# A long convolution with routed experts: output and scores by step of the last stage, one transfer for a step's tables

## The chip, the cores and the metric

The kernel runs on one core of a Trainium2 chip. The metric is the device time of one execution in microseconds, as the median of several runs. One further execution was recorded by the hardware profiler; all rows below come from that one.

## The reference

Two things are computed one after the other, for 8 sequences of 6336 positions with 128 features each.

1. A causal convolution along the sequence, each feature with its own filter: `y = irfft(rfft(x, 2S) * rfft(h, 2S))[:S]`.
2. A layer of experts on the result. Every position gets a score, `scores = y @ w_gate`. In each sequence the 128 positions with the largest scores are replaced by `y + sigmoid(score) * (relu(y @ w1) @ w2)`; `w1` is 128 x 1024 and `w2` 1024 x 128. All other positions keep `y`.

```
out = y.copy()
for b in range(8):
    top = argpartition(-scores[b], 128)[:128]
    out[b, top] += sigmoid(scores[b, top]) * (relu(y[b, top] @ w1) @ w2)
```

## The kernel before

The transform of length 6400 = 50 x 128 is done by matrix products. A sequence pair or a single sequence is worked on as a "unit"; there are 8, numbered 0 to 7. In units 0 to 5 two units belong to a pair of sequences, and each holds half of the features; units 6 and 7 are single sequences. Unit -1 is the filter.

A unit passes through four stages, all of them products on PE with copies or sums behind them:

- **a** (`products_a`, L194; copies by ACT or the DVE, L211): 8 blocks of x, each in two halves. x is loaded by `load_x` (L126), and each block is folded by two sums before use (`fold`, L133 and L134, on the DVE or POOL).
- **b** (`stage_b`, products recorded under the helper's line L109): 13 chunks. Each needs a table (`tab_wb`, L156) and the filter's spectrum (`hd`, L162 or L165). The DVE multiplies (L276 or L282), POOL adds (L287).
- **c** (`stage_c`, L300; copies by ACT, L301): 16 chunks.
- **d**, the last stage (`stage_d`, L320): 8 steps. A step takes two tables of 200 KB (`load_d`, L172, `tab_at`), makes 16 products into two banks, `pt[0]` and `pt[1]`, copies the first bank to SBUF on ACT (L324, tile `st`), and forms sum and difference on the DVE (L329, L330). Then POOL multiplies by the gate weights (L338, tile `tm`), and `rest` reduces that to scores in the tile `ss` on the DVE (L356 for units 0 to 5, L348 to L354 for units 6 and 7) and issues two stores of 200 KB on SP's queue (L359), each of 4 KB from 50 lanes. `rest` is put off to the next step (one step later still in unit 7).

The tiles `st`, `tm`, `tx`, `cmp` and a few others share one ring of 5 buffers (`wide`), so a new `st` waits until an old one has been stored. In unit 7 `st` lies elsewhere, in `reg`.

Stages of different units are interleaved by a list written ahead (`plan`): the d-steps of a unit run between the a-blocks of the unit after next (two halves of a block, then one d-step), and the c-chunks of a unit between the b-chunks of the next. In unit 6 the d-steps run between c-chunks of unit 7, and those of unit 7 alone.

All ordinary transfers are issued by SP, in the order of the program. Tables lie in a ring `wbuf` of six slots of 2 KB per lane (`room`): a d-step takes two neighbouring slots, a b-chunk two (three or none in units 6 and 7), a chunk of the filter one. `ask` looks ahead in the plan and issues loads as long as the users between the current one and the one asked for hold no more than six slots:

```
if sum(1 if o[0] == "j" else 0 if o in own else 3 if o[0] == "b" and o[1] >= SINGLE else 2
       for o in users[used:asked[0] + 1]) > 6:
    break
tabs[s] = (load_d if s[0] == "d" else load_b)(*s[1:])
```

For a d-step in the midst of its stage that means: tables are asked for two steps ahead. A load waits in SP's queue until the slot's last reader is done, and whatever stands behind it waits with it.

The search for the 128 largest scores (`keys` with L375 to L385, `search` with L416 to L505) turns scores to whole-number keys and narrows a threshold digit by digit: comparisons on the DVE (L464, L466) and ACT (L477), counts over the lanes by a small product on PE. For units 0 to 5 it runs piece by piece between the steps of later units; for units 6 and 7 serially. `places` works out the rows' numbers, POOL gathers them from the output (L622), the experts run, and POOL scatters them back (L668). The number of a row counts positions of a lane in the order in which the scores of the lane lie in `ss`, and `rows_out` views the output in the same order.

Of the kernel before, what the change touches and what calls it, by code (L numbers as in the profile page):

```python
# [7 lines left out]
F32 = mybir.dt.float32  # L8
# [4 lines left out]
ALU = mybir.AluOpType  # L13
AX = mybir.AxisListType
# [3 lines left out]
B, S, D = 8, 6336, 128  # L18
N1, N2 = 50, 128
L = N1 * N2  # L20
HD = D // 2
# [3 lines left out]
LN = 114  # L25
# [8 lines left out]
def conv_moe(ctx, tc, x, h, w_gate, w1, w2, fa_d, wb_d, wc_d, at_d, tri_d, cst_d, outs):  # L34
    nc = tc.nc
    v = nc.vector
    g = nc.gpsimd
    cp = ctx.enter_context(tc.tile_pool(name="cp", bufs=1))
# [18 lines left out]
    def single():  # L57
        return turn(banks)
# [5 lines left out]
    def wide(name):  # L64
        return tp.tile([128, 1024], F32, tag="t", name=name, bufs=5)

    def small(shape, dtype, name, bufs=1):
        return tp.tile(shape, dtype, tag=name, name=name, bufs=bufs)
# [6 lines left out]
    def sums(unit):  # L75
        t = big[:, 0:2 * 128 * HD] if unit + 1 == NU else half
        return t.rearrange("p (j r m t) -> p j r m t", j=HD, r=2, t=2)
# [9 lines left out]
    cst = cp.tile([128, 14], F32, name="cst")  # L87
# [5 lines left out]
    lane16 = (lanes16[0:LN, 0:1], lanes16[0:LN, 1:2])  # L93
    wbuf = cp.tile([128, 6 * KC * 128], F32, name="wbuf")
    hd = dp.tile([2, 128, 2 * N1 * HD], F32, name="hd")
    ss = [cp.tile([LN, 2, 2, 32], F32, name="ss%d" % i) for i in range(2)]

    def view(unit):
        if unit >= SINGLE:
# [36 lines left out]
    used_room = [0]  # L136

    def room(n):
        o = used_room[0] % 6
        used_room[0] += n  # L140
        return wbuf[:, o * 512:(o + n) * 512]
# [24 lines left out]
        return wt, [ht[:, r * kn * HD:(r + 1) * kn * HD] for r in range(2)]  # L166

    def load_d(unit, i):
        r = []
        for c in range(2):  # L170
            t = room(1)[:, 0:8 * N1].rearrange("p (c a r n) -> p c a r n", c=2, a=2, r=2)
            nc.sync.dma_start(out=t, in_=at_d[:, i, 2 * c:2 * c + 2])  # L172
            r.append(t)
        return r
# [134 lines left out]
    def flush(keep=0):  # L309
        while len(late) > keep:  # L310
            late.pop(0)()

    def stage_d(unit, i, ats):
        u, hv = unit % 2, sums(unit)
        pt = [single(), single()]
        for r in range(2):
            for c in range(4):
                for a in range(2):
                    m = 8 * i + 4 * a + c
                    nc.tensor.matmul(pt[r][a * 64:a * 64 + N1, c * 128:c * 128 + 128],  # L320
                                     ats[c // 2][0:LN, c % 2, a, r], hv[0:LN, :, r, m], start=True, stop=True)
# [12 lines left out]
        n = D if unit >= SINGLE else HD  # L334
        split = last and i > 6
        for e, o in ((g, 0), (v, 512)) if split else ((g, 0),):
            z = 512 if split else 1024
            e.tensor_tensor(out=tm[:, o:o + z].rearrange("p (a d) -> p a d", d=n),  # L338
                            in0=st[:, o:o + z].rearrange("p (a d) -> p a d", d=n),
                            in1=w.unsqueeze(1).broadcast_to([LN, z // n, n]), op=ALU.mult)  # L340

        def rest():
            if unit >= SINGLE:
                tv = tm.rearrange("p (s c d) -> p s c d", s=2, c=4)
                k = 0 if unit + 1 < NU else 3 if split else 1
                for c in range(k):
                    for a in range(1 if split else 2):
                        nc.scalar.activation(out=small([LN, D], F32, "tossed"), in_=tv[:, a, c], func=AF.Copy,  # L348
                                             accum_out=ss[u][:, 0, a, 4 * i + c:4 * i + c + 1])
                if split:  # L350
                    v.tensor_reduce(out=ss[u][:, 0, 1, 4 * i:4 * i + 4], in_=tv[:, 1], axis=AX.X, op=ALU.add)
                    v.tensor_reduce(out=ss[u][:, 0, 0, 4 * i + k:4 * i + 4], in_=tv[:, 0, k:4], axis=AX.X, op=ALU.add)
                else:
                    v.tensor_reduce(out=ss[u][:, 0, :, 4 * i + k:4 * i + 4], in_=tv[:, :, k:4], axis=AX.X, op=ALU.add)  # L354
            else:
                v.tensor_reduce(out=ss[u][:, :, :, 4 * i:4 * i + 4].rearrange("p b s c -> p s c b"),  # L356
                                in_=tm.rearrange("p (s c b d) -> p s c b d", s=2, c=4, b=2), axis=AX.X, op=ALU.add)
            for a in range(2):
                nc.sync.dma_start(  # L359
                    out=outs[unit][a, :, :, 4 * i:4 * i + 4],  # L360
                    in_=st[a * 64:a * 64 + N1].rearrange("p (s c b d) -> p s c b d", s=2, c=4, b=2))

        late.append(rest)

    def keys(units, nb, bits):

        key = small([LN, 2, nb, HD], F32, "key%d" % nb)
        tmp = spare[0:LN, 48:432] if nb == 2 else wide("keys")[0:LN, 0:384]  # L370
        tmp = tmp.bitcast(I32)
        ki, hf = tmp[:, 0:64 * nb], tmp[:, 128:128 + 128 * nb].rearrange("p (h b n) -> p h b n", h=2, b=nb)
        tot = ss[units[0] % 2][:, 0:nb].rearrange("p b s c -> p (b s c)")
        if nb == 2:
            v.tensor_tensor(out=tot, in0=tot, in1=ss[1].rearrange("p b s c -> p (b s c)"), op=ALU.add)  # L375
        raw = tot.bitcast(I32)
        v.tensor_scalar(out=ki, in0=raw, scalar1=31, scalar2=-2147483648, op0=ALU.arith_shift_right,
                        op1=ALU.bitwise_or)
        v.tensor_tensor(out=ki, in0=ki, in1=raw, op=ALU.bitwise_xor)
        kb = ki.rearrange("p (b n) -> p b n", b=nb)  # L380
        v.tensor_scalar(out=hf[:, 0], in0=kb, scalar1=bits, scalar2=2 ** (32 - bits) - 1,
                        op0=ALU.logical_shift_right, op1=ALU.bitwise_and)
        v.tensor_scalar(out=hf[:, 1], in0=kb, scalar1=2 ** bits - 1, scalar2=None, op0=ALU.bitwise_and)
        kv = key.rearrange("p h b (s c) -> p (h b) s c", s=2)
        v.tensor_tensor(out=kv, in0=hf.rearrange("p h b (s c) -> p (h b) s c", s=2),  # L385
                        in1=cst[0:LN, 5:7].unsqueeze(1).unsqueeze(3).broadcast_to([LN, 2 * nb, 2, 32]), op=ALU.mult)
        return key

    share = [7]
# [3 lines left out]
    def search(units, paced):  # L393
# [15 lines left out]
        if paced:  # L409
            key = keys(units, nb, bits)  # L410
            yield "v"
        else:
            ahead = small([LN, nt], F32, "ahead")
            limits = small([LN, 2], F32, "limits")
            v.memset(bb, 0.5)
            v.scalar_tensor_tensor(out=nth, in0=row, scalar=-float(base ** levels[0] // base),  # L416
                                   in1=bb.unsqueeze(2).broadcast_to([LN, nb, nt]), op0=ALU.mult, op1=ALU.add)
            key = keys(units, nb, bits)
            yield "v"
# [177 lines left out]

    def rows_out(unit):
        if unit >= SINGLE:
            return outs[unit].rearrange("a n s c b d -> (a n s c) (b d)")  # L600
        return outs[unit].rearrange("a n s c b d -> (a n s c b) d")

    w1s = (big[:, 16384:16896], half[:, 1024:1536])
    w2s = half[:, 0:1024]
# [25 lines left out]
    def expert(n, units, iu):  # L630
# [27 lines left out]
        def finish():  # L658
            v.scalar_tensor_tensor(out=xe, in0=py[:, 0:D], scalar=gg[:, 0:1], in1=xe, op0=ALU.mult, op1=ALU.add)
            for i, u in enumerate(units):  # L660
                back.append((rows_out(u), iu, xe[:, i * wd:i * wd + wd]))
# [71 lines left out]
    for u in range(NU):  # L733
        if u + 2 <= NU:
            both = merge(c_list(u), b_list(u + 1))
            n = next(i for i, s in enumerate(both) if s[0] == "b") + 2 * (u % 2)
# [76 lines left out]
    for s in plan:  # L813
        kind, unit = s[0], s[1]
        n = (unit + 1) * 8
# [5 lines left out]
        if kind == "a":  # L821
            q, t = s[2:]
# [22 lines left out]
        elif kind == "j":  # L845
            c = s[2]
# [8 lines left out]
            n = KCH[c][1] * HD  # L855
# [16 lines left out]
        elif kind == "c":  # L872
            stage_c(*s[1:])
            i = HALVES.index(s[2] // 2 * 2)
# [157 lines left out]
```

## Time and profile before

| | |
|---|---|
| Median of 3 runs | 797.8 us (797.77 to 798.41) |
| The profiled execution's own time | 804.7 us |
| Span of the profiled execution, first to last instruction | 802.8 us |
| Mean granted TensorE clock | 0.983 of full speed |
| PE, PEld, DVE, ACT, POOL busy | 92%, 80%, 78%, 56%, 69% of the span |
| Bytes moved | 157.64 MB, 196 GB/s on average |

The engines are PE (TensorE's products), PEld (its weight loads, beside the products), DVE (VectorE), ACT (ScalarE), POOL (GpSimd) and SP (SyncE, which only issues transfers here). Times in rows are microseconds from the start of the span; L172 is line 172 of the kernel before. In rows of the timeline, "[1.28 <-DMA wbuf<-tab_at]" says that the engine stood idle for 1.28 us just before and that a transfer into `wbuf` ended most of it; "issue" there is idle time for which the profile shows no releaser. A tile's name stands for all its buffers.

### The profile page before, as it was taken

To read this page: it belongs to the slowest core of one execution; us is meant where nothing else is said; L and a number is where in the kernel's file an instruction comes from. 1 tells how busy PE (TensorE), PEld (TensorE's weight loads), DVE (VectorE), ACT (ScalarE), POOL (GpSimd) and SP (SyncE) were. 2 spreads that over 40 slices of the span, in tenths; PEclk is the share of its full clock that TensorE was granted. 3 is DMA by queue.
4 is the path that set the end of the run, shared out by engine and by line. 5 is a ranking of instruction groups with operands and counts; after the bars stand their busy time and mean duration, and the time that the engine had idled before them with its cause. 6 is when DMAs were issued, how large, how long until landed. Compare 5 with 4: busy or idle time off the path is not lost.

```text
span 802.8 us, 39710 instructions
## 1 busy us (share of the span) xinstructions
PE 735.0 (92%) x17566; PEld 643.2 (80%) x17566; DVE 629.7 (78%) x1067; ACT 451.5 (56%) x965; POOL 551.3 (69%) x406
## 2 busy tenths in 40 slices
PE   6699979999999999999999999999999998888665
PEld 6675578888999878987889788889888888778554
DVE  5549956676767699999877898999668997975983
ACT  4687643365336546666456466655554666655562
POOL 0018928977797779877978698777885666722933
PEclk9889989999999999999999999999999999999989
DMA  7829816657865776578647774699478736521610
GB/s 268 259 83 329 267 55 215 208 166 233 261 216 160 231 261 215 155 219 273 229 126 230 256 259 123 193 331 327 126 224 267 253 110 183 171 65 31 205 54 17
DMA packets 82292, 157.64 MB, mean 196 GB/s; under 512 B 9366, under 2 KB 30088, under 8 KB 82120
## 3 DMA queue, kind: packets, MB, share of 16 engines
q1 hardware_dynamic: 81224, 154.05, 59.4%
q8 instruction: 138, 2.26, 1.1%
q0 software_dynamic: 896, 1.05, 0.5%
q14 instruction: 34, 0.28, 0.1%
HBM read 121.77 MB, written 33.29 MB: 193 GB/s over the span
## 4 chain that ended last, share of the span: by engine, by line
PE 65%; DVE 18%; issue 7%; DMA 5%; ACT 2%; POOL 1%; SPq 1%; another core or an unknown queue 0%; POOLq 0%; DVEq 0%; ACTq 0%
PE pb L300 23%; PE pt L109 17%; PE pb L320 10%; PE pt L194 10%; DVE tx L282 2%; DVE cmp L464 2%; PE pb L109 2%; PE pb L194 1%; PE pm L109 1%; DVE ss L354 1%; DVE st L329 1%; DVE st L330 1%; DMA out<-st 1%; ACT junk L477 1%; DVE st L251 1%
## 5 line engine op out<-in xcount | busy, mean ns | idle before, releaser
L301 ACT COPY half<-pb 114x512 f32<-114x512 f32 x224 | 147.0, 656 | 165.5 <-PE pb L300 161.1
L287 POOL TENSOR_TENSOR big<-big,tx 128x512 f32<-128x512 f32 (+1 forms) x104 | 132.0, 1302 | 77.5 <-DVE tx L282 68.0
L338 POOL TENSOR_TENSOR tm<-st,wg 114x1024 f32<-114x1024 f32 x56 | 133.8, 2392 | 63.4 <-DVE st L330 41.7
L287 POOL TENSOR_TENSOR reg<-reg,tx 128x512 f32<-128x512 f32 (+1 forms) x104 | 130.8, 1291 | 48.2 <-PE pb L300 28.5
L300 PE MATMUL pb<-wc,reg 128*50 128x64 f32 x4096 | 126.4, 220 | 4.1 <-issue 3.7
L300 PEld LDWEIGHTS pb<-wc,reg 128*50 128x50 f32 x4096 | 121.8, 126 | 7.7 <-issue 5.7
L300 PEld LDWEIGHTS pb<-wc,big 128*50 128x50 f32 x4096 | 118.5, 126 | 3.0 <-ACT reg L211 0.3
L300 PE MATMUL pb<-wc,big 128*50 128x64 f32 x4096 | 120.6, 219 | 0.1
L320 PE MATMUL pb<-half,wbuf 114*50 114x128 f32 x1792 | 112.2, 274 | 5.7 <-issue 2.1
L320 PEld LDWEIGHTS pb<-half,wbuf 114*50 114x50 f32 x1792 | 97.1, 123 | 12.9 <-issue 3.2
L109 PE MATMUL pt<-big,wbuf 128*64 128x256 f32 x704 | 87.4, 388 | 0.8 <-issue 0.6
L109 PE MATMUL pt<-reg,wbuf 128*64 128x256 f32 x704 | 85.1, 388 | 0.0
L211 ACT COPY reg<-pt 128x800 f32<-128x800 f32 x64 | 56.3, 928 | 44.4 <-PE pt L194 44.3
L282 DVE TENSOR_TENSOR tx<-pt,wbuf 128x1024 f32<-128x1024 f32 (+1 forms) x65 | 76.3, 1174 | 0.0
L329 DVE TENSOR_TENSOR st<-pb,st 114x512 f32<-114x512 f32 x56 | 38.6, 689 | 47.4 <-PE pb L320 32.4
L109 PEld LDWEIGHTS pt<-big,wbuf 128*64 128x64 f32 x704 | 57.7, 135 | 19.5 <-issue 1.1
L109 PEld LDWEIGHTS pt<-reg,wbuf 128*64 128x64 f32 x704 | 52.3, 135 | 20.9
L211 ACT COPY big<-pt 128x800 f32<-128x800 f32 x59 | 51.6, 931 | 22.6 <-PE pt L194 20.7
L356 DVE TENSOR_REDUCE ss<-tm 114x16 f32<-114x1024 f32 x48 | 58.4, 1216 | 7.2 <-POOL tm L338 6.5
L282 DVE TENSOR_TENSOR reg<-pt,wbuf 128x1024 f32<-128x1024 f32 (+1 forms) x39 | 45.9, 1178 | 18.6 <-PE pt L109 18.4
L194 PE MATMUL pt<-fa,big 50*64 50x100 f32 x2336 | 59.4, 249 | 0.0
L194 PEld LDWEIGHTS pt<-fa,big 50*64 50x64 f32 x2336 | 51.9, 133 | 6.3 <-issue 3.5
(175 smaller groups left out, 1206.0 us busy)
## 6 DMA issues: line engine op xcount, KB each, us to landing
wbuf<-tab_at SPq DMA_DIRECT2D x128, 200.0 KB
out<-st SPq DMA_DIRECT2D x112, 200.0 KB
wbuf<-tab_wb SPq DMA_DIRECT2D x84, 256.0 KB
wbuf<-hd SPq DMA_DIRECT2D x84, 256.0 KB
big<-in_x SPq DMA_DIRECT2D x37, 512.0 KB
half<-in_x SPq DMA_DIRECT2D x15, 512.0 KB
hd<-st SPq DMA_DIRECT2D x24, 256.0 KB
reg<-in_x SPq DMA_DIRECT2D x12, 512.0 KB
```

Of the source, the lines that this page charges most:

```text
L109: nc.tensor.matmul(out[lo:hi], w[:, lo:hi], r, **k)
L194: nc.tensor.matmul(o, w, tab[lanes, c], start=True, stop=True)
L211: nc.scalar.copy(out=o, in_=i)
L282: v.tensor_tensor(out=dst.rearrange("p h a j k t -> p k h a j t"), in0=src, in1=w, op=ALU.mult)
L287: g.tensor_tensor(out=yv[:, :, r], in0=yv[:, :, r], in1=zv[:, :, 1 - r], op=ALU.add if r else ALU.subtract)
L300: nc.tensor.matmul(pt[i2 * 64:i2 * 64 + N1, o:o + HD], w, wc[:, i2], start=True, stop=True)
L301: nc.scalar.copy(out=hv[0:LN, c * 4 + j:c * 4 + j + 2].rearrange("p j r m t -> p (j r) t m"), in_=pt[0:LN].rearrange("p (j t m) -> p j t m ...
L320: nc.tensor.matmul(pt[r][a * 64:a * 64 + N1, c * 128:c * 128 + 128], ats[c // 2][0:LN, c % 2, a, r], hv[0:LN, :, r, m], start=True, stop=True)
L329: v.tensor_tensor(out=st[:, 0:512], in0=pt[1][0:LN], in1=st[:, 512:1024], op=ALU.add)
L338: e.tensor_tensor(out=tm[:, o:o + z].rearrange("p (a d) -> p a d", d=n), in0=st[:, o:o + z].rearrange("p (a d) -> p a d", d=n), in1=w.unsq ...
L356: v.tensor_reduce(out=ss[u][:, :, :, 4 * i:4 * i + 4].rearrange("p b s c -> p s c b"), in_=tm.rearrange("p (s c b d) -> p s c b d", s=2, c ...
L464: v.tensor_tensor(out=cv, in0=cur.unsqueeze(2).broadcast_to([LN, nb, nv, HD]), in1=nth[:, :, 0:nv].unsqueeze(3).broadcast_to([LN, nb, nv, ...
```

## The change

Three things change together.

- The output of a unit is laid out as (half, lane, step, s, c, b, d) instead of (half, lane, s, step and c, b, d). What a step stores for a lane is then one run of 4 KB in DRAM, and not two of 2 KB.
- The score tile `ss` gets the same order (step, s, c) within a lane, with the reductions, the keys and the mask in L385 rewritten for it, since the rows' numbers follow it. `rows_out` and the reordering after the launch follow too.
- `load_d` loads a step's tables by one transfer of 400 KB into two neighbouring slots, unless the ring stands at its last slot; then it loads two halves as before.

```
-    ss = [cp.tile([LN, 2, 2, 32], F32, name="ss%d" % i) for i in range(2)]
+    ss = [cp.tile([LN, 2, 8, 2, 4], F32, name="ss%d" % i) for i in range(2)]
...
     def load_d(unit, i):
+        if used_room[0] % 6 < 5:
+            t = room(2)[:, 0:16 * N1].rearrange("p (c a r n) -> p c a r n", c=4, a=2, r=2)
+            nc.sync.dma_start(out=t, in_=at_d[:, i])
+            return [t[:, 0:2], t[:, 2:4]]
         r = []
         for c in range(2):
             t = room(1)[:, 0:8 * N1].rearrange("p (c a r n) -> p c a r n", c=2, a=2, r=2)
...
-                v.tensor_reduce(out=ss[u][:, :, :, 4 * i:4 * i + 4].rearrange("p b s c -> p s c b"),
+                v.tensor_reduce(out=ss[u][:, :, i].rearrange("p b s c -> p s c b"),
                                 in_=tm.rearrange("p (s c b d) -> p s c b d", s=2, c=4, b=2), axis=AX.X, op=ALU.add)
             for a in range(2):
                 nc.sync.dma_start(
-                    out=outs[unit][a, :, :, 4 * i:4 * i + 4],
+                    out=outs[unit][a, :, i],
                     in_=st[a * 64:a * 64 + N1].rearrange("p (s c b d) -> p s c b d", s=2, c=4, b=2))
...
-        kv = key.rearrange("p h b (s c) -> p (h b) s c", s=2)
-        v.tensor_tensor(out=kv, in0=hf.rearrange("p h b (s c) -> p (h b) s c", s=2),
-                        in1=cst[0:LN, 5:7].unsqueeze(1).unsqueeze(3).broadcast_to([LN, 2 * nb, 2, 32]), op=ALU.mult)
+        kv = key.rearrange("p h b (i s c) -> p (h b i) s c", s=2, c=4)
+        v.tensor_tensor(out=kv, in0=hf.rearrange("p h b (i s c) -> p (h b i) s c", s=2, c=4),
+                        in1=cst[0:LN, 5:7].unsqueeze(1).unsqueeze(3).broadcast_to([LN, 16 * nb, 2, 4]), op=ALU.mult)
...
-        return outs[unit].rearrange("a n s c b d -> (a n s c b) d")
+        return outs[unit].rearrange("a n i s c b d -> (a n i s c b) d")
...
-    args.append([nc.dram_tensor("out_%d" % u, (2, N1, 2, 32, 2, HD), F32, kind="ExternalOutput").ap()
+    args.append([nc.dram_tensor("out_%d" % u, (2, N1, 8, 2, 4, 2, HD), F32, kind="ExternalOutput").ap()
```

The reductions for units 6 and 7 (L348 to L354) and the sum of two units' scores (L375) are reindexed in the same way, with the same sizes.

## Rows read from the trace of the kernel before

**Rows 1.** The page: busy time by engine, and the chain's shares by engine.
```profile
PE 735.0 (92%) x17566; PEld 643.2 (80%) x17566; DVE 629.7 (78%) x1067; ACT 451.5 (56%) x965; POOL 551.3 (69%) x406
...
PE 65%; DVE 18%; issue 7%; DMA 5%; ACT 2%; POOL 1%; SPq 1%; another core or an unknown queue 0%; POOLq 0%; DVEq 0%; ACTq 0%
```
**Rows 2.** Timeline of PE, last stage of unit 1 (start, us, engine, line, operation).
```profile
251.53 1.60 PE L194 MATMUL pt<-fa,reg 50*64 50x100 f32 x64
253.07 1.97 PE L320 MATMUL pb<-half,wbuf 114*50 114x128 f32 x32
254.96 1.60 PE L194 MATMUL pt<-fa,reg 50*64 50x100 f32 x64
```
**Rows 3.** Stretches: us, busy time by engine (PE first), PEclk, DMA share, GB/s.
```profile
248.10:277.40 29.30, 28.02 (x775) 25.40 (x774) 18.72 (x22) 19.13 (x25) 21.31 (x12) 1.00 0.71 215
574.00:608.80 34.80, 33.26 (x932) 30.40 (x928) 23.10 (x39) 20.86 (x28) 27.22 (x16) 0.95 0.60 180
```
**Rows 4.** Timeline of SP's issues, last stage of unit 1.
```profile
254.95 1.72 SPq L172 DMA_DIRECT2D wbuf<-tab_at  x2
256.76 1.68 SPq L359 DMA_DIRECT2D out<-st  x2
258.54 1.94 SPq L172 DMA_DIRECT2D wbuf<-tab_at  x2
```
**Rows 5.** Who waited for the tables, then for the stores (us, times).
```profile
  PE pb L320: 2.7, 4
...
  ACT st L324: 9.2, 5
```
**Rows 6.** SP's instructions by line: ns min/median/max, first and last start.
```profile
L255 SPq DMA_DIRECT2D hd<-st x26: 319/418/1886, 51.8 to 97.1; - x26
...
L172 SPq DMA_DIRECT2D wbuf<-tab_at x128: 327/425/1869, 157.5 to 752.7; - x128
...
L359 SPq DMA_DIRECT2D out<-st x112: 777/809/1257, 172.4 to 699.3; - x112
```
**Rows 7.** Timeline of the DVE, last stage of unit 4.
```profile
509.72 0.69 DVE L329 TENSOR_TENSOR st<-pb,st 114x512 f32<-114x512 f32 x1 [0.16 <-ACT st L324]
```
**Rows 8.** Timeline of PE, idle times in the last stages of units 0 and 1.
```profile
180.33 1.92 PE L320 MATMUL pb<-half,wbuf 114*50 114x128 f32 x30 [0.42 <-issue]
...
194.84 1.97 PE L320 MATMUL pb<-half,wbuf 114*50 114x128 f32 x32 [0.69 <-DVE st L330]
...
272.72 1.30 PE L320 MATMUL pb<-half,wbuf 114*50 114x128 f32 x20 [1.27 <-issue]
```
**Rows 9.** Timeline of SP's issues, last stage of unit 5.
```profile
570.67 8.73 SPq L126 DMA_DIRECT2D big<-in_x  x2
579.45 3.79 SPq L172 DMA_DIRECT2D wbuf<-tab_at  x6
```
**Rows 10.** Timeline of PE, last stage of unit 5.
```profile
583.66 0.65 PE L320 MATMUL pb<-half,wbuf 114*50 114x128 f32 x8 [1.28 <-DMA wbuf<-tab_at]
584.56 2.40 PE L320 MATMUL pb<-half,wbuf 114*50 114x128 f32 x24 [0.26 <-DMA wbuf<-tab_at]
586.89 2.34 PE L194 MATMUL pt<-fa,reg 50*64 50x100 f32 x64
```
**Rows 11.** Stretch of 2 us in unit 5, columns as in group 3.
```profile
586.00:588.00 2.00, 2.00 (x38) 1.65 (x38) 0.90 (x2) 0.00 (x0) 1.32 (x2) 0.50 0.77 250
```
**Rows 12.** Timelines of SP, PE and the DVE, last stage of unit 7.
```profile
752.14 2.11 SPq L172 DMA_DIRECT2D wbuf<-tab_at  x2
...
752.96 1.96 PE L320 MATMUL pb<-big,wbuf 114*50 114x128 f32 x32 [0.67 <-DMA wbuf<-tab_at]
...
757.26 1.52 PE L320 MATMUL pb<-big,wbuf 114*50 114x128 f32 x24 [0.45 <-DMA wbuf<-tab_at]
...
758.89 0.69 DVE L329 TENSOR_TENSOR reg<-pb,reg 114x512 f32<-114x512 f32 x1 [0.36 <-ACT tossed L348]
```
**Rows 13.** The DVE's operation that masks the keys, L385: ns min/median/max.
```profile
L385 DVE TENSOR_TENSOR key<-keys,cst x2: 293/294/294, 703.4 to 764.3; 114x128 f32<-114x128 int32 x2
```

More of the change, by code (lines that the diff above doesn't have):

```diff
@@ L348, in rest @@
                         nc.scalar.activation(out=small([LN, D], F32, "tossed"), in_=tv[:, a, c], func=AF.Copy,
-                                             accum_out=ss[u][:, 0, a, 4 * i + c:4 * i + c + 1])
+                                             accum_out=ss[u][:, 0, i, a, c:c + 1])
                 if split:
-                    v.tensor_reduce(out=ss[u][:, 0, 1, 4 * i:4 * i + 4], in_=tv[:, 1], axis=AX.X, op=ALU.add)
-                    v.tensor_reduce(out=ss[u][:, 0, 0, 4 * i + k:4 * i + 4], in_=tv[:, 0, k:4], axis=AX.X, op=ALU.add)
+                    v.tensor_reduce(out=ss[u][:, 0, i, 1], in_=tv[:, 1], axis=AX.X, op=ALU.add)
+                    v.tensor_reduce(out=ss[u][:, 0, i, 0, k:4], in_=tv[:, 0, k:4], axis=AX.X, op=ALU.add)
                 else:
-                    v.tensor_reduce(out=ss[u][:, 0, :, 4 * i + k:4 * i + 4], in_=tv[:, :, k:4], axis=AX.X, op=ALU.add)
+                    v.tensor_reduce(out=ss[u][:, 0, i, :, k:4], in_=tv[:, :, k:4], axis=AX.X, op=ALU.add)
             else:
-                v.tensor_reduce(out=ss[u][:, :, :, 4 * i:4 * i + 4].rearrange("p b s c -> p s c b"),
+                v.tensor_reduce(out=ss[u][:, :, i].rearrange("p b s c -> p s c b"),
                                 in_=tm.rearrange("p (s c b d) -> p s c b d", s=2, c=4, b=2), axis=AX.X, op=ALU.add)
@@ L372, in keys @@
         ki, hf = tmp[:, 0:64 * nb], tmp[:, 128:128 + 128 * nb].rearrange("p (h b n) -> p h b n", h=2, b=nb)
-        tot = ss[units[0] % 2][:, 0:nb].rearrange("p b s c -> p (b s c)")
+        tot = ss[units[0] % 2][:, 0:nb].rearrange("p b i s c -> p (b i s c)")
         if nb == 2:
-            v.tensor_tensor(out=tot, in0=tot, in1=ss[1].rearrange("p b s c -> p (b s c)"), op=ALU.add)
+            v.tensor_tensor(out=tot, in0=tot, in1=ss[1].rearrange("p b i s c -> p (b i s c)"), op=ALU.add)
         raw = tot.bitcast(I32)
@@ L599, in rows_out @@
         if unit >= SINGLE:
-            return outs[unit].rearrange("a n s c b d -> (a n s c) (b d)")
-        return outs[unit].rearrange("a n s c b d -> (a n s c b) d")
+            return outs[unit].rearrange("a n i s c b d -> (a n i s c) (b d)")
+        return outs[unit].rearrange("a n i s c b d -> (a n i s c b) d")
     w1s = (big[:, 16384:16896], half[:, 1024:1536])
@@ L1021 @@
     o = _np.stack([r.results[0]["out_%d" % u] for u in range(NU)])
-    w = o[0:n].reshape(n // 2, 2, 2, N1, 2, 8, 4, 2, HD).transpose(0, 7, 2, 3, 4, 5, 6, 1, 8)
-    w = _np.concatenate([w.reshape(n, 2, N1, 2, 8, 4, D), o[n:].reshape(B - n, 2, N1, 2, 8, 4, D)])
+    w = o[0:n].reshape(n // 2, 2, 2, N1, 8, 2, 4, 2, HD).transpose(0, 7, 2, 3, 5, 4, 6, 1, 8)
+    ones = o[n:].reshape(B - n, 2, N1, 8, 2, 4, D).transpose(0, 1, 2, 4, 3, 5, 6)
+    w = _np.concatenate([w.reshape(n, 2, N1, 2, 8, 4, D), ones])
     y = _np.zeros((B, N1, N2, D), o.dtype)
```

## Prediction

> **What bounds the kernel now.** I read the parts by engine and by chain first. The span is 802.8 us, PE is busy for 735.0 of it, and the chain of work that ended last runs through PE for 65% and through DMA for 5% [rows 1]. The change touches nothing of PE's work, only stores, table loads and the order of 64 scores in a lane, so its gain can only come out of the few stretches in which PE or the DVE waits for SP's queue. To find them I read the stretches that hold the last stage, which runs 8 steps per unit (a step here: two products of the unit after next, L194, and then the 16 products of the last stage, L320).
>
> A step without a stall takes 3.43 us: L194 starts at 251.53 and again at 254.96 [rows 2]. Eight of them are 27.4 us. In the stretch of unit 1 PE is busy 28.02 of 29.30 us, in that of unit 5, the longest, 33.26 of 34.80 [rows 3]. So all that such a stage could give back is 1 to 2 us, unit 5 apart.
>
> Next SP's queue, in order of time. In these stages it issues without a pause: two table loads 1.72 us, two stores 1.68 us, the next two loads 1.94 [rows 4]. That is 3.4 to 3.6 us a step, PE's own pace, so SP, once late, stays late. The reader should see that SP is nearly as full as PE, and that this alone costs nothing: what counts is who waits for what it issues. Waits of PE for the tables are four in the whole span, 2.7 us together. Waits for the stores fall on ACT, which needs an st buffer back: five, 9.2 us [rows 5].
>
> **The change, part by part.**
>
> *Stores (L359), 128 of them.* Each moves the same 200 KB; a lane's 4 KB become one run instead of two of 2 KB. Its issue costs SP 777 ns at least and 809 at the median, where a store of 128 lanes with one run each (hd) costs 418 and a table load 425 [rows 6]. The new store has one run per lane, so I take 418 ns. Its bounds are 319, the lowest of the hd store, and 809, if the price hangs on the 50 lanes and not on the runs. Two stores per step: 0.84 us for 1.68. A page of the Trainium skill speaks against the change here: "DMA: Bandwidth & Descriptors", section "Why a DMA increments its semaphore by 16 and not by 1", says that a transfer runs on the largest number of engines, up to 16, that divides the slowest dimension of both sides. By that rule 50 lanes run on 10 engines before and after, and a price that hangs on the lanes would stay: 1.68 us a step, the first rival below. No row here tells engines apart.
>
> *Table loads (L172), 128 of them.* Two of 200 KB become one of 400 KB where two neighbouring slots of the ring of six are left. Counting the slots through the plan (1 for a "j", 2 for a "b" or "d", 3 or none for a "b" of units 6 and 7), the ring stands at its last slot in three steps of every unit but unit 5: 21 steps stay split, 43 are merged, and 85 issues remain. Merged: 425 ns for about 1.7 us of back-to-back issue, bounds 327 and 1,700 (the time for the bytes of both). SP's step falls from 3.4 or more to 0.84 + 0.43 = 1.3 us, at worst 1.68 + 1.7 = 3.4, as now. The price: the first half can't start before both slots are free, nor be used before all 400 KB are there. SP waits for the second slot anyway before it goes on, so only the landing counts. In an undisturbed stage tables are asked for two steps ahead, 6.9 us; that is the cover. Where SP was blocked it is gone, which is unit 5, below.
>
> *Where late stores cost.* ACT's 9.2 us come mostly in units 2 and 4, where the search keeps the DVE busy. Behind a copy that one of these waits held up, the DVE had stood idle for 0.16 us [rows 7]. It is the DVE's own list of work that PE then waits for, and an earlier store doesn't shorten it. I take 0.2 us for all, bounds 0 and 0.9 (0.16 and the 0.69 that PE waits for DVE's L330 in unit 0 [rows 8]).
>
> *Stalls of PE with no releaser.* 0.42 us in unit 0 and 1.27 in unit 1 are marked "issue" [rows 8]: the profile shows nothing that they wait for, so I give the change nothing of them; bounds 0 and 1.7.
>
> *Unit 5, second step.* SP's queue was in the x loads from 570.67 to 579.40, held there by the second, and issued the tables of three steps from 579.45 [rows 9]. PE was ready at 582.4, got the first half at 583.66 and the second at 584.56 [rows 10]. The clock then fell: 24 pieces of L320 took 2.40 us (0.10 each, against 1.97 for 32, 0.062 each [rows 2]), 64 of L194 2.34 against 1.60, at a granted clock of 0.50, the lower level of 1.2 GHz, in 586 to 588 [rows 10, 11]. Merged, the block in the x loads stays, and the tables' bytes queue behind the same x load. The whole lands about when the second half did, 0.2 us earlier for one issue less, but the 8 pieces that ran on the first half (0.65 us) now run after it. Net +0.4 us; bounds -0.5 and +1.9 (second rival).
>
> *Unit 7.* SP issues the last step's tables at 752.14 for 2.11 us, and PE's last 24 pieces wait 0.45 us for them, the step before 0.67 [rows 12]. With SP at 1.3 us a step both go. But the DVE is full there: before the last sum it stood idle 0.36 us [rows 12]. So 0.4 us of the 1.1 reach the end, with 0.36 taken; bounds 0 and 1.1. The search that follows is serial, so this lies on the path in full.
>
> *Scores.* The order inside a lane changes from (s, i, c) to (i, s, c); all sums and compares keep their sizes. Only L385 walks in runs of 4 instead of 32, five times, 294 ns in units 6 and 7 and on the path there once [rows 13]. Taken 0; bounds 0 and +0.3, doubling it. Gathers and scatters at the end address rows of the same size.
>
> **Sum.** -0.2 (stores) +0.4 (unit 5) -0.4 (unit 7) = -0.2 us, to which I add half of PE's stall of 0.69 in unit 0 and nothing else: -0.5 us. The profiled execution took 804.7 us (its span and 1.9 around it), so 804.2; the median of the runs is 797.8, 0.9% below, and the same 0.5 us leaves 797.3. What covers the 2 us of issue that each step saves is PE, 96% busy in the stage; were PE faster, SP would be the next in line.
>
> **Rivals.**
>
> *Stores no cheaper (no effect).* If the issue price belongs to the 50 lanes, a store stays at 0.81 us and only the loads gain. SP still drops to 2.1 us a step. Against it: nothing but the two rows of 128 lanes. The time is then 797.8 less half of the 0.5, 797.6.
>
> *SP's relief is paid in full (faster).* If the late tables, the st buffers and the unexplained stalls all hang on the full queues, then 2.7 (tables) + 0.92 and 0.74 (pieces at the lower clock, 2.40 - 1.48 and 2.34 - 1.60) + 0.69 + 1.69 = 6.7 us are to be had. Half of it, 3.4, gives 794.4. For it: SP is full and every one of these stalls lies in the last stage. Against it: only 2.7 us are put down to tables, and the DVE covers part. The same page's section "Rules for kernel authors" asks to coalesce many small transfers into large ones, and so speaks for this case; no row here shows how much it is worth.
>
> *The merged table comes late (slower).* In unit 5 nothing covers the load. If 400 KB land later than 585.5, 1 us after the second half now, PE loses this 1.0, and the 8 pieces that ran ahead now cost 0.8 at the lower clock: +1.8 us. With unit 7's gain at its bound of 0 that is 799.6, and up to 801 if the third step's tables, next in the queue, are late as well. For it: the wait is at the worst place, behind an x load of 512 KB. Against it: the bytes ahead of the second half are the same as now.
>
> **How the numbers follow.** A measurement of this kernel tells 0.2%, 1.6 us, from no change. Forecast 797.3 with 0.34 and the rival without cheaper stores with 0.12 lie within it: same 0.46. Paid in full 0.36: faster. Late merged table 0.18: slower. The bounds of the terms add up to -4.2 (0.9 + 1.7 + 0.5 + 1.1) and +2.2 (1.9 + 0.3) around 797.8, so 793.6 to 800.0. I take 794.0 to 800.0; what lies past 794.4 in the second rival and the far end of the third stay outside. The forecast's own range is 796.2 to 799.4.
>
> **What would show it.** Right: stores with one run issue in about 0.42 us, 85 table loads, SP with pauses in the last stages, the stage of unit 1 still at 29 us, PE's waits for tables in unit 7 gone, DVE there as full as now. Wrong: the stage of units 0 to 4 shorter by over 1 us each, PE's "issue" stalls gone, or the clock at the higher level through unit 5. A wait at 583 that grew past 3 us would show the slow rival.

## The result, and the profile after

The changed kernel takes 803.45 us (median of 22 runs, 795.34 to 808.81) where the kernel before takes 797.79 us in the same number of runs (789.73 to 800.18). The ratio is 1.006, with a 95% interval of 1.0036 to 1.0084: it is slower, by about 5 us. The ratio leaves out the two longest runs of the changed kernel (808.33 and 808.81 us), which count as a slow state; the medians of all runs stand at 1.007. The prediction was 797.3 us in a range of 794.0 to 800.0. Both the sign and the range were wrong.

One warning before the rows. Single executions of either kernel differ by 10 us and more. The profiled execution of the changed kernel took 799.85 us, 3.6 us below its median; that of the kernel before took 804.7, 6.9 us above. So the two spans (798.1 and 802.8 us) stand the wrong way round, and a comparison of whole profiles would call the change a gain. What can be compared is stages, and what recurs over many profiles.

In the changed kernel L194 is L198, L320 is L324, L324 is L328, L359 is L363, L385 is L389; the merged table load is L171 and the split one L176. First the page's parts 1 and 4 of the changed kernel, against [rows 1]:

```profile
PE 732.4 (92%) x17566; PEld 634.8 (80%) x17566; DVE 629.2 (79%) x1067; ACT 451.9 (57%) x965; POOL 551.4 (69%) x406
...
PE 66%; DVE 18%; issue 6%; DMA 5%; ACT 3%; POOL 1%; SPq 0%; POOLq 0%; DVEq 0%; ACTq 0%
```

Nothing shows at this distance. SP's instructions by line (ns min/median/max) say that the issue became cheap, as forecast [rows 6]:

```profile
L171 SPq DMA_DIRECT2D wbuf<-tab_at x43: 327/363/1883, 158.1 to 740.8; - x43
...
L176 SPq DMA_DIRECT2D wbuf<-tab_at x42: 327/363/1722, 158.5 to 745.4; - x42
...
L363 SPq DMA_DIRECT2D out<-st x112: 285/326/1749, 170.5 to 698.9; - x112
```

SP's timeline of unit 1 after, against [rows 4], has the pauses too: a merged load and two stores are 1.1 us of a step of 3.43. Over the whole of that stage SP is issuing for 24.0 of 27.7 us before and for 12.9 of 25.8 after.

```profile
251.06 0.69 SPq L363 DMA_DIRECT2D out<-st  x2
252.53 1.49 SPq L176 DMA_DIRECT2D wbuf<-tab_at  x2
254.48 0.69 SPq L363 DMA_DIRECT2D out<-st  x2
256.40 0.36 SPq L171 DMA_DIRECT2D wbuf<-tab_at  x1
257.92 0.75 SPq L363 DMA_DIRECT2D out<-st  x2
```

PE's step in that stage is what it was [rows 2]; its timeline:

```profile
252.86 1.60 PE L198 MATMUL pt<-fa,reg 50*64 50x100 f32 x64
254.39 1.97 PE L324 MATMUL pb<-half,wbuf 114*50 114x128 f32 x32
256.29 1.60 PE L198 MATMUL pt<-fa,reg 50*64 50x100 f32 x64
```

The waits (total us, times, longest) show that ACT waits half as long for the stores [rows 5], and PE somewhat longer for the tables (POOL's waits for stores, not among those rows, went the other way, from 3.5 to 8.2 us):

```profile
ACT st L328 <- DMA out<-st: 4.8, 4, 2.4
PE pb L324 <- DMA wbuf<-tab_at: 3.5, 3, 2.3
```

PE's timeline in the last stages of units 0 to 5 holds what had not been foreseen: six idle times marked "issue", 4.8 us together, where the kernel before had three (0.42, 1.27 [rows 8] and one of 0.21).

```profile
173.52 0.90 PE L198 MATMUL pt<-fa,big 50*64 50x100 f32 x28 [0.19 <-issue]
...
188.57 0.91 PE L198 MATMUL pt<-fa,big 50*64 50x100 f32 x30 [0.97 <-issue]
...
420.74 0.65 PE L324 MATMUL pb<-half,wbuf 114*50 114x128 f32 x8 [0.75 <-issue]
...
431.26 0.47 PE L198 MATMUL pt<-fa,big 50*64 50x100 f32 x9 [1.46 <-issue]
...
509.77 0.40 PE L198 MATMUL pt<-fa,big 50*64 50x100 f32 x7 [0.85 <-issue]
...
599.45 0.39 PE L198 MATMUL pt<-fa,big 50*64 50x100 f32 x3 [0.57 <-issue]
```

In unit 5 SP is blocked in the x loads for as long as before [rows 9], and PE waits for the whole merged table [rows 10]; in this execution the clock stayed up (PEclk, the third figure from the end in the row of the stretch, is 1.00 where it was 0.95 [rows 3]):

```profile
570.58 8.71 SPq L126 DMA_DIRECT2D big<-in_x  x2
579.39 2.84 SPq L171 DMA_DIRECT2D wbuf<-tab_at  x3
...
584.60 1.96 PE L324 MATMUL pb<-half,wbuf 114*50 114x128 f32 x32 [2.35 <-DMA wbuf<-tab_at]
586.50 1.60 PE L198 MATMUL pt<-fa,reg 50*64 50x100 f32 x64
...
574.00:608.80 34.80, 31.89 (x934) 29.26 (x930) 23.13 (x40) 21.03 (x28) 27.36 (x16) 1.00 0.63 193
```

In unit 7 one of the two waits for tables is left, 0.51 us, and the DVE's last sum starts without a pause [rows 12]; the masking of the keys costs the same [rows 13]:

```profile
746.95 4.01 PE L324 MATMUL pb<-big,wbuf 114*50 114x128 f32 x64 [0.51 <-DMA wbuf<-tab_at]
...
752.60 0.68 DVE L333 TENSOR_TENSOR reg<-pb,reg 114x512 f32<-114x512 f32 x1
...
754.04 1.86 DVE L342 TENSOR_TENSOR reg<-reg,wg 114x512 f32<-114x512 f32 x1
...
L389 DVE TENSOR_TENSOR key<-keys,cst x2: 291/292/293, 703.6 to 758.5; 114x128 f32<-114x128 int32 x2
```

And the DMA queues (packets, MB, share of 16 engines' span), first the kernel before, then the changed one: 15% fewer packets in q1, the queue of SP's transfers, and the same share of time. The queue q8, whose kind is "instruction", will be needed below.

```profile
q1 hardware_dynamic: 81224, 154.05, 59.4%
q8 instruction: 138, 2.26, 1.1%
```

```profile
q1 hardware_dynamic: 68632, 154.05, 59.4%
q8 instruction: 138, 2.26, 1.1%
```

### The profile page after: what moved, and what is told of

The parts are those of the page before. It is cut to its first block, busy times and chain, and to the rows that moved or that the text cites. A ratio compares the mean times of both kernels' runs of the same rounds, so it can differ in the third digit from the quotient of the medians.

```text
span 798.1 us, 39624 instructions
## 1 busy us (share of the span) xinstructions
PE 732.4 (92%) x17566; PEld 634.8 (80%) x17566; DVE 629.2 (79%) x1067; ACT 451.9 (57%) x965; POOL 551.4 (69%) x406
## 3 DMA queue, kind: packets, MB, share of 16 engines
q1 hardware_dynamic: 68632, 154.05, 59.4%
## 4 chain that ended last, share of the span: by engine, by line
PE 66%; DVE 18%; issue 6%; DMA 5%; ACT 3%; POOL 1%; SPq 0%; POOLq 0%; DVEq 0%; ACTq 0%
PE pb L304 22%; PE pt L109 17%; PE pt L198 11%; PE pb L324 11%; DMA wbuf<-tab_at 2%; DVE cmp L468 2%; DVE tx L286 2%; PE pb L109 2%; ACT junk L481 2%; PE pb L198 1%; PE pm L109 1%; DVE ss L358 1%; DVE st L333 1%; DVE st L334 1%; DMA out<-st 1%
## 5 line engine op out<-in xcount | busy, mean ns | idle before, releaser
L342 POOL TENSOR_TENSOR tm<-st,wg 114x1024 f32<-114x1024 f32 x56 | 133.9, 2394 | 65.6 <-DVE st L334 43.2
L304 PE MATMUL pb<-wc,reg 128*50 128x64 f32 x4096 | 123.1, 220 | 2.2 <-ACT st L328 2.2
L304 PEld LDWEIGHTS pb<-wc,reg 128*50 128x50 f32 x4096 | 119.2, 126 | 5.6 <-ACT st L328 2.9
L324 PE MATMUL pb<-half,wbuf 114*50 114x128 f32 x1792 | 110.6, 273 | 5.3 <-DMA wbuf<-tab_at 3.0
L324 PEld LDWEIGHTS pb<-half,wbuf 114*50 114x50 f32 x1792 | 96.2, 122 | 11.5 <-DMA wbuf<-tab_at 2.5
L109 PEld LDWEIGHTS pt<-big,wbuf 128*64 128x64 f32 x704 | 50.6, 135 | 24.3 <-DVE tx L286 0.6
L198 PE MATMUL pt<-fa,big 50*64 50x100 f32 x2336 | 61.1, 250 | 4.2 <-issue 4.0
L198 PEld LDWEIGHTS pt<-fa,big 50*64 50x64 f32 x2336 | 52.8, 133 | 11.3 <-issue 8.5
```

The source lines that it names most:

```text
L109: nc.tensor.matmul(out[lo:hi], w[:, lo:hi], r, **k)
L198: nc.tensor.matmul(o, w, tab[lanes, c], start=True, stop=True)
L304: nc.tensor.matmul(pt[i2 * 64:i2 * 64 + N1, o:o + HD], w, wc[:, i2], start=True, stop=True)
```

## The experiments

Each kernel was timed in 12 runs on one chip beside 17 to 35 runs of the kernel before; ratios are to that. "R" below stands for the 4 KB runs, "U" for the merged table of unit 5's second step.

**The change again, and its two halves.** Theory A: the merged tables land late. Theory B: stores that are issued so fast crowd the transfers, PE's own supply among them. The halves: the diff without `load_d`'s four lines (e2), and these four lines alone (e3).

> The change as it is, again, beside its two halves on one chip. All theories: slower than the kernel before by 0.3 to 0.9% (the 22 runs gave a ratio of 1.006). It gives the yardstick for the two runs beside it and a second profile: theory A (the merged tables land late) expects PE to wait over 2 us for tables in unit 5's second step again; theory B (stores that issue in a third of the time crowd the transfers) expects PE's idle time marked issue in the last stages of units 0 to 5 at 4 us or more, against 1.9 before.

> The new layout of output and scores alone, with each step's tables in two transfers as before. Theory A (the loss is the merged tables landing late): no slower than the kernel before, 0 to -2 us, with the table wait in unit 5 at 1.3 + 0.3 us as before. Theory B (the loss is the stores: issued in 0.33 us instead of 0.81, SP no longer spaces the transfers, and loads and PE's own supply queue behind them): slower by 4 to 6 us, all of the change's loss.

> The merged table transfers alone, with output and scores laid out as before. Theory A (merged tables land late): slower by 4 to 6 us, with PE's table waits over 4 us in the span (2.7 before). Theory B (the stores): within 1 us of the kernel before.

Measured: the change 1.0078 (1.0038 to 1.0118); the layout alone 1.0031 (1.0 to 1.0062); the tables alone 1.0045 (1.0012 to 1.0077). Neither theory holds alone: the halves come out at about 2.5 and 3.5 us and add up to the whole, though the interval of the layout alone reaches down to 1.0. The traces bear out each theory in part. The change had 4.8 us of "issue" stalls again (theory B expected 4 or more) and a wait of 1.91 us in unit 5 (theory A expected over 2); with the tables alone PE's waits for them come to 2.0 us (theory A expected over 4).

The layout alone has the "issue" stalls, 6.9 us of them in the last stages; these are the three of unit 1 in its PE timeline:

```profile
264.66 1.41 PE L194 MATMUL pt<-fa,reg 50*64 50x100 f32 x50 [1.50 <-issue]
...
269.98 0.73 PE L194 MATMUL pt<-fa,big 50*64 50x100 f32 x19 [0.83 <-issue]
...
276.21 1.31 PE L320 MATMUL pb<-half,wbuf 114*50 114x128 f32 x20 [1.27 <-issue]
```

The tables alone have few of them (1.4 us), but the long wait in unit 5, and there the clock fell: 32 pieces took 3.50 us instead of 1.96.

```profile
583.50 3.50 PE L324 MATMUL pb<-half,wbuf 114*50 114x128 f32 x32 [1.97 <-DMA wbuf<-tab_at]
```

**What about the stores?** Either the runs of 4 KB, or the pace at which a step's two stores are issued. f1 stores each half in two transfers of 2 KB runs; f2 keeps the 4 KB runs and spaces the two stores.

```
f1:         for a in range(2):
+               for z in range(2):
                    nc.sync.dma_start(
-                       out=outs[unit][a, :, i],
+                       out=outs[unit][a, :, i, z],
-                       in_=st[a * 64:a * 64 + N1]...)
+                       in_=st[a * 64:a * 64 + N1, z * 512:z * 512 + 512]...)
f2: -       for a in range(2): store(a)
    +       store(0)
    +       spaced.append(lambda: store(1))    # issued behind the next ask
```

> New layout, tables as before, but each half of a step is stored by two transfers of 100 KB (2 KB runs, one per lane and transfer) instead of one of 200 KB with 4 KB runs. The bytes and the place in SP's queue are those of the new layout with whole stores (which took 1.0031 of the time before, 2.5 us); SP issues four stores a step instead of two. Theory C, the 4 KB runs hold up the fetch of PE's instructions: the 2 KB runs give that back, ratio 0.999 to 1.001 to before, PE's idle time marked issue in the last stages of units 0 to 5 back to about 2 us from 6.9. Theory D, it is the pace (a step's 400 KB reach the engines at once when two issues take 0.65 us): four issues of about 0.33 us take 1.3 us, near the 1.6 before, so about half of the loss goes, 1.001 to 1.002, issue stalls 3 to 5 us. If neither, it stays at 1.003 with 7 us of stalls.

> New layout with whole 4 KB runs, tables as before, but the second store of a step is put off until after the next request for tables, so that the two stores of a step are not issued back to back. Theory D (pace): stalls marked issue fall from 6.9 us to 2 or 3 and the ratio to before is 0.999 to 1.001. Theory C (run length): nothing changes, 1.002 to 1.005 and 5 to 8 us of issue stalls. The later store may hold an st buffer longer: then ACT's waits for it grow by up to 5 us, which costs PE under 0.5 us.

Measured: f1 0.9995 (0.9965 to 1.0026), f2 1.0055 (1.0018 to 1.0092). The loss goes with the 4 KB runs and does not go with spacing: theory C of the two. What these two do not separate is the length of the runs from the pace of a single store: SP issues 200 KB in 0.33 us with 4 KB runs, in 0.65 us in f1 (two issues of 327 ns) and in 0.81 us before. "4 KB runs" stands for both below.

```profile
L360 SPq DMA_DIRECT2D out<-st x224: 285/327/1760, 167.6 to 697.5; - x112
```

But neither profile fell in line with its time. f1 had 4.4 us of "issue" stalls in this execution and f2 only 3.0; the longest of each, from PE's timelines:

```profile
428.46 0.65 PE L194 MATMUL pt<-fa,big 50*64 50x100 f32 x12 [1.91 <-issue]
```

```profile
264.02 0.73 PE L194 MATMUL pt<-fa,big 50*64 50x100 f32 x20 [1.65 <-issue]
```

One profile counts two to ten of these stalls, so it takes many profiles to compare kernels by them. That is done below.

**What about the tables?** f3 is e3 with unit 5's second step split as before. f4 leaves layout and tables as before and moves one x load behind the request for that step's tables.

```
f3: +  if used_room[0] % 6 < 5 and (unit, i) != (5, 1):
f4: +  if s == ("d", SINGLE - 1, 0):          # behind ask(used)
    +      load_x((SINGLE + 2) * 8 + 6)
...
    -  if unit == SINGLE and s[2] in (9, 11):
    -      load_x((unit + 2) * 8 + s[2] // 2 + 1)
    +  if unit == SINGLE and s[2] == 9:
    +      load_x((unit + 2) * 8 + 5)
```

> Old layout and stores, tables merged as in the change except in the second step of unit 5, which loads two halves as before. Theory E, the cost of the merged tables (1.0045 of the time before, 3.5 us) lies in that step behind the blocked x load: the ratio falls to 0.999 to 1.001, and the wait of PE there is 1.3 us plus 0.3 again. Theory F, the cost is spread over all stages (400 KB in one queue, clock falls elsewhere): 1.003 to 1.005 as with all merged.

> The kernel before, with one x load (the sixth of unit 7) issued later, in unit 5's first step behind that step's request for tables, so that the tables of unit 5's second step no longer stand behind an x load that waits for its buffer. If the stall there (1.28 + 0.26 us) and the lower clock behind it (0.9 + 0.7 us) hang on that: 2 to 3 us less, ratio 0.996 to 0.998. If PE then waits for that x block instead, or the fall of the clock comes from elsewhere: 0.999 to 1.002.

Measured: f3 1.0011 (0.998 to 1.0043), f4 1.0023 (0.9993 to 1.0053). f3 lies nearer to theory E, but its interval holds theory F's 1.003 too. In f3 PE again waits as in the kernel before, and the clock stayed up (1.53 us for 24 pieces):

```profile
577.37 0.65 PE L324 MATMUL pb<-half,wbuf 114*50 114x128 f32 x8 [1.14 <-DMA wbuf<-tab_at]
578.41 1.53 PE L324 MATMUL pb<-half,wbuf 114*50 114x128 f32 x24 [0.40 <-DMA wbuf<-tab_at]
```

f4 did not come out as expected. Its SP timeline shows why: a second x load (the one that block 0 of unit 7 asks for) still stood blocked ahead of the tables and was let go only at 575.13, so PE waited 0.78 and 0.71 us.

```profile
575.13 0.33 SPq L126 DMA_DIRECT2D big<-in_x  x1
575.51 2.39 SPq L172 DMA_DIRECT2D wbuf<-tab_at  x4
...
579.25 0.65 PE L320 MATMUL pb<-half,wbuf 114*50 114x128 f32 x8 [0.78 <-DMA wbuf<-tab_at]
580.61 1.53 PE L320 MATMUL pb<-half,wbuf 114*50 114x128 f32 x24 [0.71 <-DMA wbuf<-tab_at]
```

**Do the mends add up?** The whole change with f1's stores and f3's line (g1), with f1's stores alone (g2), with f3's line alone (g4).

> The whole change with two mends at once: each half of a step is stored in two transfers of 2 KB runs, and the tables of unit 5's second step are loaded in two halves; all other tables stay merged. The whole change took 1.006 and 1.0078 of the time before. If the loss is the 4 KB runs (mended alone: 0.9995) plus the late table in unit 5 (mended alone: 1.0011): 0.999 to 1.002. If these two single results were luck and the loss sits elsewhere (400 KB transfers, order of the scores, the code): still 1.005 or more.

> The whole change with only the stores mended (2 KB runs, four issues a step). If the two costs add: what is left is the table's part, 1.002 to 1.004, and PE waits 1.5 to 2.4 us for the table in unit 5. If the 4 KB runs are the whole loss: 0.999 to 1.001. If they are none of it: 1.005 to 1.008.

> The whole change with only unit 5's second step mended (its tables in two halves; stores stay at two issues of 4 KB runs). If the two costs add: what is left is the stores' part, 1.002 to 1.004, PE's wait in unit 5 back at about 1.5 us with the first 8 pieces ahead, and its issue stalls in the last stages at 4 to 7 us. If the merged table is the whole loss: 0.999 to 1.001. If it is none of it: 1.005 to 1.008.

Measured: g1 1.004 (1.001 to 1.007), g2 1.0049 (1.002 to 1.0078), g4 1.0065 (1.0026 to 1.0104). All lie below e1's 1.0078, but g1 lies above what was expected: something of 0.2 to 0.4% was left. g4's single ratio shows nothing of its mend, and its "issue" stalls (2.9 us) stayed below the 4 to 7 expected. g2 lies between two of its expectations; in it PE waited longest of all for the merged table (1.5 to 2.4 us had been expected), and the clock fell behind it:

```profile
583.64 3.66 PE L324 MATMUL pb<-half,wbuf 114*50 114x128 f32 x32 [3.45 <-DMA wbuf<-tab_at]
```

**Both x loads out of the way.** f5 is f4 with the second x load moved as well, to the same place; h1 is f5 with the tables merged everywhere, unit 5 included.

```
f5: f4, and
+      load_x((SINGLE + 2) * 8 + 7)           # at ("d", SINGLE - 1, 0)
...
-  if unit >= 2 and (q, t) == (0, 1):
+  if 2 <= unit < NU - 1 and (q, t) == (0, 1):
       load_x(n + 7)
```

> The kernel before with the last two x loads of unit 7 (moving one alone left the other in the way and gave 1.0023) both issued behind the request for tables in unit 5's first step. The tables of the second step are then issued before 575 us and nothing blocked stands ahead of them. If the stall there (1.28 + 0.26 us) goes and is not replaced: 1.5 us less, 3 us where the lower clock followed, ratio 0.996 to 0.999. If PE then waits for the x blocks, or the gain is lost in other stalls: 0.999 to 1.003.

> Old layout and stores, all tables merged as in the change (including unit 5's second step), and the last two x loads of unit 7 issued behind unit 5's request for tables. The eleven timed kernels so far fit a sum of parts (as shares of the time before): 4 KB runs +0.36%, merged table in unit 5's second step +0.23%, the other merged tables +0.19%, the new order alone 0, x loads later -0.21%. If the merged table in unit 5 costs because the x load is ahead of it, that cost goes as well: 0.19 - 0.21, ratio 0.998 to 1.001, and no wait for the table of 1 us or more there. If it costs wherever it stands, 0.19 + 0.23 - 0.21: 1.001 to 1.004 and a wait of over 1 us remains.

Measured: f5 0.9985 (0.9953 to 1.0018), h1 0.998 (0.9947 to 1.0013). In f5, SP issues the tables ahead of the x loads, and PE comes to its second step at 580.79 without a wait:

```profile
566.76 7.75 SPq L172 DMA_DIRECT2D wbuf<-tab_at  x6
574.56 3.33 SPq L126 DMA_DIRECT2D big<-in_x  x2
...
579.26 1.60 PE L194 MATMUL pt<-fa,reg 50*64 50x100 f32 x64
580.79 1.97 PE L320 MATMUL pb<-half,wbuf 114*50 114x128 f32 x32
```

In h1 the merged tables do the same:

```profile
568.40 6.56 SPq L171 DMA_DIRECT2D wbuf<-tab_at  x3
...
579.95 1.60 PE L198 MATMUL pt<-fa,reg 50*64 50x100 f32 x64
581.48 1.97 PE L324 MATMUL pb<-half,wbuf 114*50 114x128 f32 x32
```

h1 and e3 differ by these two x loads alone, and stand 0.65% apart (0.998 and 1.0045). In the traces the wait for the merged table goes with the blocked x load ahead of it, and not with the merging. That the cost in time does so too is likely but not shown: the intervals of h1 and e3 just touch, and the same two x loads also take 0.15% off the kernel with split tables (f5). Both f5 and h1 are faster than the changed kernel; that either beats the kernel before is likely but not shown, as both intervals hold 1.

**All comparisons together.** Single ratios are uncertain by 0.3%. The thirteen comparisons (twelve experiments and the first result) were fitted by a sum of parts, on the means of the runs that the ratios rest on, each weighted by its scatter; the table gives share and standard error, and us at 800:

```
new layout by itself               +0.04% +- 0.08    0.3
4 KB runs (R)                      +0.28% +- 0.09    2.2
merged tables but for unit 5's     +0.17% +- 0.08    1.4
merged table in unit 5's 2nd (U)   +0.19% +- 0.09    1.6
both x loads later                 -0.27% +- 0.10   -2.2
second store spaced (f2 only)      +0.09% +- 0.18    0.7
one x load later (f4 only)         +0.12% +- 0.12    1.0
```

The parts of the change add up to 5.5 us (0.68%). No comparison lies further from the fit than 0.8 of its own errors. The 4 KB runs are told from nothing, at three times their error, and so are the merged tables taken together (0.37% +- 0.07). How the latter divide between unit 5's second step and all others is open, as each part is only about twice its error; h1, which has the merged tables, is as fast as f5, which has not.

The profiles, one of each kernel, show the place of the first part. The last stages of units 0 to 4, each from its first last-stage product to the first product after it, taken from PE's timeline, are in sum:

```
with 4 KB runs:     after 139.5, e1 141.3, e2 142.2, f2 139.9, g4 137.3    mean 140.0
without:            before 137.7, e3 137.2, f1 139.7, f3 135.7, f4 135.8,
                    g1 134.5, g2 138.3, f5 138.0, h1 137.6                 mean 137.2
issue stalls, units 0 to 5: with 2.9 to 6.9, mean 4.5; without 0.8 to 4.4, mean 2.2
unit 5's last stage: merged behind the x load (after, e1, e3, g2) 29.1 to 32.8, mean 30.6;
                     split behind it (before, e2, f1, f2, f3, g1, g4) 28.0 to 31.7, mean 29.5;
                     x loads later (f5, h1) 26.7, 27.6
```

The 4 KB runs cost 2.8 us in the last stages of units 0 to 4 (standard error 1.0), which covers their price in the fit (2.2), and the "issue" stalls grow by 2.2 us (standard error 0.8): most of it.

The merged tables are less clear. In units 0 to 4 they cost nothing: without 4 KB runs, these stages take 136.7 us in mean with merged tables and 137.8 with split ones. Unit 5's last stage as a whole is 1.1 us longer with the merged table behind the x load, at a standard error of 0.9. Closer up, from the moment at which PE is ready for unit 5's second step to the end of its products, it takes 4.24, 3.80, 5.40 and 7.04 us (after, e1, e3, g2), against 3.50 to 4.51 where the tables are split, and 1.90 in f5 and h1, where nothing is waited for. The clock fell there in three profiles: e3, g2 and before. In the others the merged step takes 4.0 us in mean and the split one 3.7. In unit 6's last stage kernels with merged tables take 33.7 us, the others 33.4 (f1 33.8). The rest of the tables' price in the fit has no place that these profiles show.

What are these stalls? In the record of the transfers, the instruction queue q8 moves 138 packets of 16 KB in an execution, one for about 127 of PE's 17566 products. In all fourteen profiles, each "issue" stall of 0.3 us or more in these stages ended 1.3 to 1.6 us after such a packet had landed, and they come at places that lie 127 products apart, or a multiple of that, within a few products: the reading that fits is that PE had run out of instructions. The 0.69 us in unit 0 that the profile puts down to the DVE [rows 8] is one too, 1.64 us behind its packet. That the instructions are late because of the 4 KB runs is likely; how the one holds up the other is not shown. PE passes such a place every 127 products or so, and the next packet starts 1.6 to 2.1 us after that on average in the last stages of the five profiles with 4 KB runs, and 1.4 to 1.9 us after it in the nine others. The means, 1.9 and 1.6, point the same way (standard error of the difference 0.1), but the ranges overlap.

## Why the prediction was wrong

By its own steps:

- **What bounds the kernel.** "Its gain can only come out of the few stretches in which PE or the DVE waits for SP's queue" was right, and no gain came. The text then asked only what could be gained there; but for the late table of unit 5 it had no sentence on what a stage in which PE is 96% busy can lose when the transfers change. Its one sign of a slower kernel, a wait at 583 past 3 us, did not show (2.35 us).
- **Stores' issue.** Forecast 418 ns, bounds 319 and 809; measured 326. The first rival (stores no cheaper) is refuted: the price did not hang on the 50 lanes. f1 says the same: its stores have 50 lanes and 2 KB runs, and cost 327 ns. The prediction had argued for that rival from the rule on the number of engines in the Trainium skill's page "DMA: Bandwidth & Descriptors", section "Why a DMA increments its semaphore by 16 and not by 1", by which 50 lanes run on ten engines. The trace agrees with that rule, if each engine that takes part closes with one packet of 4 bytes: f1's 128 further stores of 50 lanes come with 1280 more of these in q1 than the 8790 before, ten each, and the 43 loads of 128 lanes that the change saves take away 688, sixteen each. But the number of engines does not set SP's time: it is the same at 809 and at 326 ns.
- **Table loads.** 85 issues were forecast and 43 + 42 are there, at 363 ns (425 forecast). SP's step fell to 1.1 us (1.3 forecast).
- **"Where late stores cost", -0.2 us.** ACT's waits for stores halved, 9.2 to 4.8 us; they are 0.6 to 6.8 us in the eight profiles with the new layout and 7.6 to 10.4 in the six with the old. No gain from it can be told in the times: the new layout with 2 KB runs (f1), which has it too, is at 0.9995.
- **"Stalls of PE with no releaser": the step that failed.** It read "the profile shows nothing that they wait for, so I give the change nothing of them; bounds 0 and 1.7". The lower end was a gain of nothing; a loss was left out with no reason given. What the runs showed in its place: these stalls end behind packets of the instruction queue, and kernels with 4 KB runs have 2.2 us more of them in their last stages (standard error 0.8) and take 2.2 us longer (fit, 0.8). The half of PE's 0.69 us in unit 0 that the sum counted as a gain belongs here too: it was such a stall and no wait for the DVE. This term takes the forecast of 797.3 to 799.5, and the merged tables (1.6 us for 0.4 in unit 5, 1.4 for 0 elsewhere) to 802.1, out of the range; how 4 KB runs would make instructions late stays open.
- **Unit 5, second step, +0.4 us.** The mechanism was as told: the x load blocks, the whole table lands late, the 8 pieces that ran ahead run behind. In the profiles in which the clock stayed up the step is 0.4 us longer merged than split, as forecast. By the fit it costs 1.6 us (standard error 0.7), within the bound of 1.9. The waits in the merged kernels are 2.35, 1.91, 1.97 and 3.45 us, against 1.14 + 0.40 to 1.80 in those that split, and the clock fell behind two of the four, against one of seven split ones, which is too few to tell. The forecast had read the clock's fall from one execution [rows 10]. The third rival's price of 1.8 us came out near the fit's, but not by its mechanism: a table that lands 1 us later than the second half did. From the issue of the step's first table to the end of PE's wait it took 5.21, 4.78, 4.83 and 6.32 us (after, e1, e3, g2), against 5.11 for the second half before; only in g2 was it late.
- **The other merged tables, 0.** They cost 1.4 us by the fit (standard error 0.6), or nothing by h1. "In an undisturbed stage tables are asked for two steps ahead, 6.9 us; that is the cover" held in the main: unit 2's stage shows one wait of 0.68 us in the changed kernel, and one of 0.54 to 0.78 in e1, g2 and h1, which have merged tables too.
- **Unit 7, -0.4 us.** The wait of 0.45 and the DVE's pause of 0.36 went as forecast: from the start of the products at 750.32 before and 744.47 after, the DVE's last sum of the first bank comes 8.57 and 8.13 us later. The gain was lost in the next operation: the DVE's multiplication (L338, now L342) took 1.40 us before and 1.86 after, so that L385 comes 14.01 and L389 14.02 us behind that start. That is not the work of the change, as this operation takes 1.83 to 1.87 us in all later profiles, f4's and f5's among them, but f1's (1.25). From the first product of this stage to the masking of the keys it takes 26.20 to 26.23 us in nine of the fourteen profiles, before and after among them, with PE waiting up to 1.07 us for tables (g4) or not at all (e2), and 27.2 to 27.9 in the five others. So these waits were not on the path, and what was counted as a gain never was one.
- **Scores, 0.** Right: 292 ns for 294, and the layout by itself costs 0.3 us with an error of 0.6.
- **"SP's relief is paid in full"**, the rival with the highest chance (0.36), is refuted: SP has its pauses, and nothing that it was said to hold up came back. The Trainium skill's page "DMA: Bandwidth & Descriptors", section "Rules for kernel authors", which asks to coalesce many small transfers, spoke for it; this trace shows no transfer time gained. In the last stage of unit 1 a packet of 2 KB takes 84 ns at the median and one of 4 KB 159, so two short ones are worth 168: the bytes take nearly as long, and q1's share of time stayed at 59.4%.

## What to carry to other kernels

A stall for which the profile names no releaser can still hang on the transfers: compare where it ends with the packets of the instruction queue, and give it a bound on the side of the loss as well. Fewer and longer transfers took work off the queue that issues them, which was worth nothing here, as that queue was not what was waited for. A longer transfer that stands behind a blocked one costs what its first half used to hide; moving the blocked one took the whole wait away (f5, h1), splitting the long one did not (f3). Where runs scatter by 1%, no single profile decides: vary the parts in several kernels and fit all of them.

## What the runs showed of the hardware

- An instruction queue moves a packet of 16 KB for about every 127 products of PE, and PE's stalls without a releaser, up to 1.9 us long in these runs (f1), end 1.3 to 1.6 us after one has landed. The number of products (17566) is the same in all kernels.
- SP's time for a store of 50 lanes of 4 KB is 326 ns where DRAM holds one run for a lane, and 809 where it holds two; f1's 327 ns for 100 KB in one run for a lane says that it goes with the runs and not with the bytes.
- A wait of 2.35 us was followed by a granted clock of 1.00 (after), and one of 1.28 + 0.26 by 0.50 (before): the length of the wait alone doesn't tell which of the two levels follows.
